# One decode kernel: the first pair's keys in one load, wo's row read by two engines, gu's half rows behind down's first block

## The chip, the core and the metric

The kernel runs on one core of one Trainium2 chip, whose other cores it leaves idle. The metric is device microseconds of one execution, the median of several. The kernel before takes 680.18 us (three runs, 679.79 to 680.27). One further execution was taken with the hardware profiler; its own time is 679.98 us and its span, first instruction to last, 678.2 us. All times of single instructions below are from that execution, counted from the start of its span.

## What is computed

One token passes through one transformer block whose two layer norms are scaled and shifted by a condition vector:

```python
mod = silu(c) @ w_mod                      # six rows of 640: sa, ca, ga, sb, cb, gb
h = layernorm(x) * (1 + ca) + sa
x = x + ga * A(h)                          # A: q = h @ wq; softmax(q k / sqrt(128)) v; @ wo
h = layernorm(x) * (1 + cb) + sb
x = x + gb * ((silu(h @ w_gate) * (h @ w_up)) @ w_down)
```

The width is 640. Attention has 32 heads of 128 with a cache of 16384 positions, and each head has its own keys and values, in bf16. Keys and values are 134 MB each, of 290 MB read in all. The feed-forward width is 1728, which is 13 chunks of 128 and one of 64.

## The kernel before, in words

**The plan.** All instructions are written as operations with an engine, a name and a list of operations that they depend on (`op` and `dma`, L77 and L83). Each engine gets its operations in the order in which the program names them, and waits on semaphores for those of other engines. So a wait on an engine holds up everything named later on that engine. All large loads are issued by SyncE (SP in the profile) at L90, one after another in the program's order, each one when its dependencies are met.

**Heads in pairs.** The 32 heads are 16 pairs. A pair's keys are 8192 KB, 64 KB on each of 128 partitions, and so are its values. There are two key buffers (`kring`, slots 0 and 1) and one value buffer (`vbuf`). The last pair's values go into key slot 0. Before the pairs start, `w_mod` lies in key slot 1 and `wq` in `vbuf`, so their users have to be done before K1 (pair 1's keys) and V0 (pair 0's values) can be loaded. K0 goes straight into slot 0.

**One pair.** VectorE (DVE) multiplies the keys by the query (mult) and folds the products in halves (fold). TensorE (PE) sums the remaining 16 columns against an identity (R). VectorE finds the largest score (pm), ScalarE (ACT) and TensorE spread it (d2, mx), VectorE takes the minimum (nb), and ScalarE does the exponential (exp, L602). Then TensorE multiplies by the values (pv, L518). A pair is worked in two parts. For pairs 1 to 14 (`score`, L549) the parts are halves of each head's 128 elements, so both need the whole load. For the first and the last pair (`score_end`, L567) the parts are the two halves of the positions, with the cut in `KCUT`.

**The order of the loads.** SyncE issues w_mod, wq, K0 in two loads of 4096 KB, K1, V0, and then K2, V1, K3, V2 and so on. K(p+1) waits until R of pair p-1 is done in both parts (its slot is free then), and V(p) waits until pv of pair p-1 is done. pv(p-1) stands in TensorE's order behind the first R of pair p, and this R needs the first mult and folds of pair p. VectorE's order over the first pairs is: mult and three folds of pair 0's first part, the same of its second part, mult of pair 1's first part, pm of pair 0, first fold, nb of pair 0, second fold, mult and folds of pair 1's second part, mult of pair 2.

**The tail.** Behind the last pair come wo's projection, the second layer norm, gate and up, and down. wo (L683 to L690) is 64 matmuls of 32 weight columns each: for each of 32 chunks one matmul with 512 columns into `wr_ps[0]` and one with 128 into `wr_ps[1]`, on four column groups of the array in turn. ScalarE copies both results into `wo_row` (L693), ten small matmuls (`wo_cols`, L699) turn the row into columns, and everything behind needs them. `gu` (L754) is the product of gate and up, `down` (L760 to L774) is five blocks of w_down: 16, 16, 16, 4 and 4 matmuls, each with its own load (wd0 to wd4). The last block is the chunk of 64, whose rows are spread over 128 partitions as half rows. `twice_gu` (L755, TensorE) and `gu_half` (L757, VectorE) make its factor.

Of the kernel before, what the change touches and what calls it, by code (L numbers as in the profile page):

```python
# [8 lines left out]
ALU = mybir.AluOpType  # L9
ACTF = mybir.ActivationFunctionType  # L10
# [27 lines left out]
class _Plan:  # L38
# [38 lines left out]
    def op(self, eng, fn, deps=(), name="", chan=None):  # L77
        o = _Op(eng, fn, list(deps), name, len(self.ops), self.loop.get(eng), chan)
        o.sig = chan is not None
        self.ops.append(o)  # L80
        return o

    def dma(self, out_ap, in_ap, key, deps=(), name="", eng="sp", noncontig=False):  # L83
        nc = self.nc

        def fn(e, out_ap=out_ap, in_ap=in_ap, noncontig=noncontig):
            if noncontig:
                with nc.allow_non_contiguous_dma(reason="tiny vector layout change"):
                    return e.dma_start(out_ap, in_ap)
            return e.dma_start(out_ap, in_ap)  # L90

        return self.op(eng, fn, deps, name, chan=self.dma_chan(key))
# [126 lines left out]
def build(nc, A_x, A_k, A_v, A_wq, A_wo, B_wg, B_wu, B_wd, c_in, w_mod, out):  # L219
    H, S, Dh = A_k.shape[1], A_k.shape[2], A_k.shape[3]  # L220
    D = A_x.shape[2]
# [4 lines left out]
    T2 = 2 * S // 128  # L226
# [4 lines left out]
    NF = 13  # L231
# [4 lines left out]
    FCH = NF + 1  # L236
# [6 lines left out]
    with es:  # L243
        block = es.enter_context(nc.Block())
        plan = _Plan(nc, es)
        op, dma = plan.op, plan.dma
        POOL, ACT, DVE, PE = "pool", "act", "dve", "pe"

        def sb(name, shape, dtype):
            return es.enter_context(nc.sbuf_tensor(name, list(shape), dtype))  # L250
# [62 lines left out]
        gu_col = sb("gu_col", [128, FCH], BF16)  # L313
        gu_half = sb("gu_half", [128, 2], BF16)
        even = sb("even", [128, 2], F32)
        twice = sb("twice", [128, 64, 2], BF16)
# [5 lines left out]
        wo_row = q_f[:, 0:2 * D].bitcast(F32)  # L322
# [11 lines left out]
        wr_ps = [psb[1], psb[6]]  # L334
        cx_ps = psb[4]
        A_ps = psb[6]
        attn_ps = psb[7]
# [23 lines left out]
            out=ident[:], in_=ones_bf[:], pattern=[[1, 128]], compare_op=ALU.is_equal,  # L361
# [27 lines left out]
        def layernorm_ops(src_f32, src_dep, sum_ap, c0, tag, xc_t, free=None, between=None):  # L389
# [26 lines left out]
            out=sel[:], in_=ident[:].rearrange("p (s r) -> p r s", s=4)[:, 0:8, :], axis=AX.X, op=ALU.add), deps=[o_ident], name="sel")  # L416
        o_msk = op(DVE, lambda e: e.tensor_reduce(
            out=msk[:], in_=ident[:].rearrange("p (j k) -> p j k", k=32), axis=AX.X, op=ALU.add), deps=[o_ident], name="msk")

        def f_e32(e):  # L420
# [3 lines left out]
        o_even = op(DVE, lambda e: e.tensor_reduce(  # L424
            out=even[:], in_=ident[:].rearrange("p (j k) -> p k j", k=2), axis=AX.X, op=ALU.add), deps=[o_ident], name="even")
        o_twice = op(DVE, lambda e: e.tensor_copy(out=twice[64:128], in_=ident[64:128, 64:128].unsqueeze(2).broadcast_to([64, 64, 2])), deps=[o_ident], name="twice")
# [4 lines left out]
        def wide(col):  # L431
            return col.broadcast_to([col.shape[0], 32])
# [11 lines left out]
        def pick(half, n, o_m, free):  # L444
# [13 lines left out]
            out=tt1[:], in0=modc[:, KC:2 * KC], scalar=1.0, in1=xn[:], op0=ALU.add, op1=ALU.mult),  # L458
            deps=[o_m0, o_xn], name="t1")
# [11 lines left out]
        for g in range(H // 4):  # L471
            b = g % 2
# [9 lines left out]
            for half in range(2):  # L482
                ps = slice(64 * half, 64 * half + 64)
                ev.append(op(ACT, lambda e, g=g, b=b, half=half, ps=ps: e.activation(
                    out=qbc[ps, 2 * g:2 * g + 2, :],
                    in_=q_ps[b][ps, :].rearrange("p (a h d) -> p a h d", a=2, h=2)[:, :, half, :], func=ACTF.Copy),
                    deps=[o_q[g]], name="qbc%d_%d" % (g, half)))
# [6 lines left out]
        KCUT = [0, T2 // 2, T2]  # L494
# [2 lines left out]

        def load_k(p):
            deps = [o_R[p - 2]] if p >= 2 else ([o_mod[1]] if p == 1 else [])
            cuts = KCUT if p == 0 else [0, T2]  # L500
            d_k[p] = [dma(kring[:, p % 2, a:b], k_src(p)[:, a:b], ("k", p % 2, c), deps=deps, name="dma_k%d_%d" % (p, c))
                      for c, (a, b) in enumerate(zip(cuts, cuts[1:]))]

# [106 lines left out]
        def step(p):  # L610
# [3 lines left out]
            diag(p - 1)  # L614

        load_k(0)
        load_k(1)
        load_v(0)
        reduce_end(0, 0, score_end(0, 0))
# [22 lines left out]
        f1 = score_end(PL, 1)  # L642
# [11 lines left out]
        for i, (b, r0, r1) in enumerate(DOWN):  # L654
            if b is None:
                dst, src = wt_v, B_wd[NF * 128:F, :].rearrange("q (h n) -> (q h) n", h=2)
            else:
# [7 lines left out]
                 deps=[o_exp[PL], o_rz, o_onesf, o_rstd], name="L")  # L665
# [5 lines left out]
            out=Z[:].rearrange("p (h j) -> p h j", j=4), in0=msk[:].unsqueeze(1).broadcast_to([128, H, 4]),  # L671
            in1=on_f[:].unsqueeze(2).broadcast_to([128, H, 4]), op=ALU.mult), deps=[o_on, o_msk], name="z")
        o_am = op(PE, lambda e: e.matmul(A_ps[:, 0:H], lhsT=Z[:], rhs=e32[:], start=True, stop=True),
                  deps=[o_z, o_e32] + o_qev[-2], name="am")
# [3 lines left out]
            out=Z[:].rearrange("p (j k) -> p j k", k=32), in_=msk[:].unsqueeze(2).broadcast_to([128, 4, 32])), deps=[o_msk, o_am], name="strips")  # L678

        def project(c):  # L680

            def f_wo(e):
                last = None  # L683
                for k in range(WCUT[c], WCUT[c + 1]):
                    r = k % 4
                    for ps, a, b in ((wr_ps[0], 0, 512), (wr_ps[1], 512, D)):
                        last = e.matmul(ps[32 * r:32 * r + 32, 0:b - a], lhsT=wide(A_sb[:, k:k + 1]), rhs=wo_v[:, k, a:b],  # L687
                                        start=(k < 4), stop=(k >= H - 4), tile_position=(0, 32 * r))
                return last
            return op(PE, f_wo, deps=[o_as, d_wo[c], o_exp[NP - 2]] + o_qev[-1], name="wo%d" % c)  # L690
        for c in range(len(WCUT) - 1):
            o_p = project(c)
        o_wr = [op(ACT, lambda e, a=a, b=b, ps=ps: e.activation(out=wo_row[:, a:b], in_=ps[:, 0:b - a], func=ACTF.Copy),  # L693
                   deps=[o_p, f1], name="wo_row%d" % a) for ps, a, b in ((wr_ps[0], 0, 512), (wr_ps[1], 512, D))]

        def f_cols(e):
            last = None
# [9 lines left out]
        o_abf = op(DVE, lambda e: e.tensor_copy(out=attn_bf[:], in_=attn_ps[:, 0:KC]), deps=[o_wo], name="attn_bf")  # L707
        o_ga = op(DVE, lambda e: e.tensor_tensor(out=tt2[:], in0=attn_bf[:], in1=ga, op=ALU.mult), deps=[o_abf, o_m0], name="ga_attn")
        o_x1 = op(DVE, lambda e: e.scalar_tensor_tensor(
            out=x1[:], in0=tt2[:], scalar=1.0, in1=x_f32[:], op0=ALU.mult, op1=ALU.add, accum_out=st[:, 4:5]),  # L710
            deps=[o_ga, o_xf], name="x1")
# [18 lines left out]
        def gate0(o_xc1):  # L730
# [5 lines left out]
            out=tt3[:], in0=xc1[:], scalar=st[:, 7:8], in1=onep_b[:], op0=ALU.mult, op1=ALU.mult),  # L736
            deps=[o_xc1, o_rstd1, o_onep_b], name="t2")
# [3 lines left out]
            out=x1_sp.rearrange("p (r k) -> p r k", k=KC), in0=x1[:].unsqueeze(1).broadcast_to([128, 32, KC]),  # L741
            in1=e32[:].unsqueeze(2).broadcast_to([128, 32, KC]), op=ALU.mult), deps=[o_x1, o_e32, o_diag[PL]], name="x1_sp")
        o_xr = op(PE, lambda e: e.matmul(xr_ps[:, 0:RW], lhsT=Z[:], rhs=x1_sp, start=True, stop=True),
                  deps=[o_xsp, o_ot[PL], o_strips], name="x1_rows")
# [7 lines left out]
        o_sg = op(DVE, lambda e: e.tensor_tensor(out=sg[:], in0=g_sb[:], in1=rg[:], op=ALU.mult), deps=[o_rg, o_gs], name="sg")  # L752
        o_x1r = op(ACT, lambda e: e.activation(out=x1_row, in_=xr_ps[:, 0:RW], func=ACTF.Copy), deps=[o_xr], name="x1_row")
        o_gum = op(DVE, lambda e: e.tensor_tensor(out=gu_col[:], in0=u_ps[:, 0:FCH], in1=sg[:], op=ALU.mult), deps=[o_sg, o_u], name="gu")  # L754
        o_tw = op(PE, lambda e: e.matmul(attn_ps[:, 8:9], lhsT=twice[64:128].rearrange("p q h -> p (q h)"), rhs=gu_col[64:128, NF:FCH], start=True, stop=True),  # L755
                  deps=[o_gum, o_twice, o_abf], name="twice_gu")
        o_guh = op(DVE, lambda e: e.tensor_tensor(out=gu_half[:], in0=attn_ps[:, 8:9].broadcast_to([128, 2]), in1=even[:], op=ALU.mult),  # L757
                   deps=[o_tw, o_even], name="gu_half")

        for i, (b, r0, r1) in enumerate(DOWN):  # L760

            if b is None:
                work = [(gu_half[:, r // 2:r // 2 + 1], wt_v[:, RW * (r % 2):RW * (r % 2) + RW], r) for r in range(4)]
            else:
                j0 = BLOCKS[b][2]
                work = [(gu_col[:, j:j + 1], wd_v[:, j, RW * r:RW * r + RW], r) for j in range(j0 + r0, j0 + r1) for r in range(4)]

            def f_down(e, i=i, work=work):
                last = None
                for at, (col, rows, r) in enumerate(work):  # L770
                    last = e.matmul(f_ps[32 * r:32 * r + 32, 0:RW], lhsT=wide(col), rhs=rows, start=(i == 0 and at < 4),  # L771
                                    stop=(i == len(DOWN) - 1 and at >= len(work) - 4), tile_position=(0, 32 * r))
                return last
            prev = op(PE, f_down, deps=[o_gum if b is not None else o_guh, d_wd[i], o_nb[PL]], name="down%d" % i)  # L774
        o_t3 = op(DVE, lambda e: e.tensor_tensor(out=tt_row, in0=f_ps[:, 0:RW], in1=gb_row[:], op=ALU.mult), deps=[prev, o_gb], name="gb_ffn")
        o_or = op(DVE, lambda e: e.tensor_tensor(out=o_row[:], in0=tt_row, in1=x1_row, op=ALU.add), deps=[o_t3, o_x1r], name="o_row")
        o_dst = out[0, 0].rearrange("(r n) -> r n", r=4)
# [51 lines left out]
```

## Time and profile before

| What | Value |
|---|---|
| Median of three runs | 680.18 us (679.79 to 680.27) |
| The profiled execution's own time | 679.98 us |
| Its span | 678.2 us |
| VectorE busy | 513.0 us (76%) |
| TensorE busy in matmuls | 366.2 us (54%) |
| ScalarE busy | 46.7 us (7%) |
| HBM read | 290.47 MB, 428 GB/s over the span |
| The queue that carries the loads (q1) | 99.2% of 16 engines' span |

The landing of one load is its issue (timeline of SyncE) plus the time from issue to landing that the view of the issuing line gives for that issue alone:

| Load | Issued | Issue to landing | Landed |
|---|---|---|---|
| w_mod, 4800 KB | 0.8 | 14.2 | 15.0 |
| wq, 5120 KB | 1.3 | 25.9 | 27.2 |
| K0, first 4096 KB | 1.73 | 35.1 | 36.9 |
| K0, second 4096 KB | 2.2 | 45.4 | 47.6 |
| K1, 8192 KB | 19.3 | 47.7 | 67.0 |
| V0, 8192 KB | 38.9 | 47.5 | 86.4 |
| K2, 8192 KB | 74.0 | 31.8 | 105.8 |
| V1, 8192 KB | 99.2 | 25.9 | 125.1 |
| K3, 8192 KB | 108.5 | 36.0 | 144.5 |
| V2, 8192 KB | 134.0 | 29.8 | 163.8 |

How to read it: the 16 DMA engines work through the loads in the order of issue. An issue whose time to landing is well over what its bytes take has waited behind others, which means that the engines had work all along.

### The profile page before, as it was taken

Reading aid. Unit: us, or ns where it says so; the run is one execution under the profiler, and the core shown is the slowest. Engines: PE = TensorE matmul, PEld = TensorE weight load, DVE = VectorE, ACT = ScalarE, POOL = GpSimd, SP = SyncE. Lnnn points to the kernel's source line nnn. Section 1 sums busy time; section 2 is a strip of 40 time slices with the busy share of each in tenths; the row PEclk is TensorE's granted clock in tenths of the full one; section 3 lists DMA queues with packets and bytes.
Section 4 is the critical chain, followed back from the end, with each engine's and each line's share of the span. In section 5 each row is a group of like instructions: output and inputs, shape, how many; then the busy total and the mean of one; then the engine's idle time right before and its main releaser. Section 6 shows DMA issues by size and latency. Waiting matters only on the chain.

```text
span 678.2 us, 5410 instructions
## 1 busy us (share of the span) xinstructions
PE 366.2 (54%) x2068; PEld 146.5 (22%) x2069; DVE 513.0 (76%) x185; ACT 46.7 (7%) x147; POOL 0.7 (0%) x6
## 2 busy tenths in 40 slices
PE   2522275755728274664818375572818465471677
PEld 1111122221312122221302122121212222130236
DVE  2189997959596896959597795959699695959812
ACT  1120000100000000000000010000000000000011
POOL 0000000000000000000000000000000000000000
PEclk9675565655657565565757555575756556575765
DMA  9999999999999999999999999999999999999997
GB/s 372 442 459 433 433 433 430 433 430 433 437 430 433 433 433 433 433 437 433 433 433 433 437 433 433 433 433 433 433 433 433 433 433 433 433 437 433 434 402 305
DMA packets 6355, 290.58 MB, mean 428 GB/s; under 512 B 714, under 2 KB 972, under 8 KB 1484
## 3 DMA queue, kind: packets, MB, share of 16 engines
q1 hardware_dynamic: 6340, 290.48, 99.2%
q8 instruction: 5, 0.08, 0.0%
q10 hardware_dynamic: 8, 0.00, 0.0%
q14 instruction: 2, 0.02, 0.0%
HBM read 290.47 MB, written 0.00 MB: 428 GB/s over the span
## 4 chain that ended last, share of the span: by engine, by line
DMA 48%; DVE 28%; issue 13%; PE 11%; DVEq 0%; ACT 0%; SPq 0%
DMA kring<-in_A_k_cache_dram 45%; DVE kring L554 10%; PE psb L544 7%; DVE kring L559 6%; DVE kring L570 4%; DVE kring L576 3%; DMA vbuf<-in_A_wo_dram 3%; DVE kring L564 3%; PE psb L518 1%; PE psb L724 1%; PE psb L687 1%; PE psb L584 1%; PE psb L699 0%; PE psb L771 0%; DVE pm L590 0%
## 5 line engine op out<-in xcount | busy, mean ns | idle before, releaser
L554 DVE TENSOR_TENSOR kring<-kring,qbc 128x16384 bf16<-128x16384 bf16 x28 | 243.2, 8687 | 96.2 <-DMA kring<-in_A_k_cache_dram 96.2
L544 PE MATMUL psb<-kring,ident 128*128 x448 | 197.5, 607 | 119.3 <-DVE kring L564 119.3
L559 DVE TENSOR_TENSOR kring<-kring 128x8192 bf16<-128x8192 bf16 x28 | 123.8, 4420 | 0.5
L544 PEld LDWEIGHTS psb<-kring,ident 128*128 128x128 bf16 x448 | 53.9, 120 | 247.1 <-issue 246.0
L518 PE MATMUL psb<-vbuf,PZ 128*8 128x512 bf16 x960 | 82.6, 520 | 0.0
L594 PE MATMUL psb<-d,bd_f 128*128 128x64 f32 x32 | 11.0, 446 | 122.0 <-ACT d L592 122.0
L564 DVE TENSOR_TENSOR kring<-kring 128x4096 bf16<-128x4096 bf16 x28 | 64.0, 2286 | 0.5
L570 DVE TENSOR_TENSOR kring<-kring,qbc 128x16384 bf16<-128x16384 bf16 x4 | 34.8, 8688 | 23.4 <-DMA kring<-in_A_k_cache_dram 23.4
L518 PEld LDWEIGHTS psb<-vbuf,PZ 128*8 128x8 bf16 x960 | 27.0, 109 | 60.2 <-issue 51.5
L584 PE MATMUL psb<-kring,ident 128*128 128x128 bf16 x64 | 14.5, 392 | 40.3 <-DVE kring L576 40.3
L594 PEld LDWEIGHTS psb<-d,bd_f 128*128 128x128 f32 x32 | 8.0, 311 | 124.1 <-DVE pm L590 114.4
L576 DVE TENSOR_TENSOR kring<-kring 128x8192 bf16<-128x8192 bf16 (+2 forms) x12 | 31.7, 2645 | 0.3
L533 PEld LDWEIGHTS psb<-sel,acc_sb 128*128 128x128 f32 x128 | 28.5, 311 | 8.4 <-issue 4.3
L533 PE MATMUL psb<-sel,acc_sb 128*128 128x2 f32 x128 | 25.6, 322 | 1.4 <-ACT acc_sb L524 1.4
L524 ACT ACTIVATE acc_sb<-psb 128x512 f32<-128x512 f32 x16 | 9.6, 597 | 212.0 <-PE psb L518 212.0
L602 ACT ACTIVATE PZ<-psb,nb 64x256 bf16<-64x256 f32 x32 | 15.0, 469 | 64.8 <-DVE nb L598 64.6
L584 PEld LDWEIGHTS psb<-kring,ident 128*128 128x128 bf16 x64 | 7.4, 122 | 46.7 <-DVE kring L576 41.6
L592 ACT ACTIVATE d<-negid,pm 128x64 f32<-128x64 f32 x16 | 5.6, 348 | 153.9 <-DVE pm L590 153.9
L477 PE MATMUL psb<-vbuf,h_col 128*128 128x512 bf16 x39 | 11.2, 461 | 8.3 <-DMA vbuf<-in_A_wq_dram 8.3
L537 ACT ACTIVATE OT_sb<-psb 128x2 f32 (+1 forms) x16 | 2.8, 172 | 151.3 <-PE psb L533 151.3
L590 DVE TENSOR_REDUCE pm<-psb 128x1 f32<-128x256 f32 x16 | 6.7, 418 | 3.7 <-PE psb L584 3.7
L477 PEld LDWEIGHTS psb<-vbuf,h_col 128*128 128x128 bf16 x40 | 4.3, 116 | 15.6 <-DMA vbuf<-in_A_wq_dram 8.8
(104 smaller groups left out, 80.4 us busy)
## 6 DMA issues: line engine op xcount, KB each, us to landing
kring<-in_A_k_cache_dram SPq DMA_DIRECT2D x2, 4096.0 KB, 40.3
vbuf<-in_A_wq_dram SPq DMA_DIRECT2D x1, 5120.0 KB, 25.9
kring<-in_w_mod_dram SPq DMA_DIRECT2D x1, 4800.0 KB, 14.2
vbuf<-in_A_wo_dram SPq DMA_DIRECT2D x1, 4480.0 KB, 23.0
kring<-in_B_w_gate_dram SPq DMA_DIRECT2D x1, 2160.0 KB, 18.7
kring<-in_B_w_up_dram SPq DMA_DIRECT2D x1, 2160.0 KB, 23.5
kring<-in_B_w_down_dram SPq DMA_DIRECT2D x3, 640.0 KB, 25.7
vbuf<-in_A_wo_dram SPq DMA_DIRECT2D x1, 640.0 KB, 24.2
```

Of the source, the lines that this page charges most:

```text
L477: last = e.matmul(q_ps[b][:, 0:512], lhsT=h_col[:, k:k + 1].broadcast_to([128, 128]), rhs=wq_v[:, k, g * 512:(g + 1) * 512], start=(k == 0 ...
L518: last = e.matmul(acc_ps[32 * s:32 * s + 8, :], lhsT=PZ[:, j, :], rhs=v_at(p)[:, 4 * j:4 * j + 4, :].rearrange("p t d -> p (t d)"), start= ...
L533: last = e.matmul(OT_ps[:, 0:2], lhsT=acc_sb[:, 128 * i:128 * (i + 1)], rhs=sel[:, i:8:4], start=(i == 0), stop=(i == 3))
L544: last = e.matmul(S_ps[:, 0:T2], lhsT=ident[:], rhs=kring[:, bass.ds(plan.slot(p), 1), :, d].rearrange("p o t -> p (o t)"), start=(d == 0) ...
L554: return e.tensor_tensor(out=kv4, in0=kv4, in1=q4, op=ALU.mult)
L559: o_f = op(DVE, lambda e: e.tensor_tensor(out=kv4[:, :, 0], in0=kv4[:, :, 0], in1=kv4[:, :, 1], op=ALU.add), deps=[o_m], name="fold%d_%d" ...
L564: return op(DVE, lambda e: e.tensor_tensor(out=lo[:, :, 0:QR], in0=lo[:, :, 0:QR], in1=lo[:, :, QR:QW], op=ALU.add), deps=[o_f], name="fol ...
L570: o = op(DVE, lambda e: e.tensor_tensor(out=kv, in0=kv, in1=qbc[:, p, :].unsqueeze(1).broadcast_to([128, KCUT[c + 1] - KCUT[c], 128]), op= ...
L576: o = op(DVE, lambda e, w=w: e.tensor_tensor(out=kv[:, :, 0:w], in0=kv[:, :, 0:w], in1=kv[:, :, w:2 * w], op=ALU.add), deps=[o], name="fol ...
L584: last = e.matmul(S_ps[:, KCUT[c]:KCUT[c + 1]], lhsT=ident[:], rhs=kring[:, p % 2, KCUT[c]:KCUT[c + 1], d], start=(d == 0), stop=(d == 15))
L594: o_mx[p] = op(PE, lambda e: e.matmul(mx_ps[:, 0:64], lhsT=bd_f[:], rhs=d2[:], start=True, stop=True), deps=[o_d2, o_bd1, o_bd2, o_nb[p - ...
L602: o_exp[p] = op(ACT, lambda e, half=half, ps=ps: e.activation(out=PZ[ps, :, 4 * half:4 * half + 4], in_=S_ps[ps, 0:T2].rearrange("p (c i) ...
```

## The change

Three edits. K0 is one load of 8192 KB instead of two of 4096 KB; its two parts are still computed one after the other with the cut of `KCUT`, and both now wait for the one load. wo's two results are 320 columns each, the first copied by ScalarE and the second by VectorE, instead of 512 and 128 columns that ScalarE copies one after the other. `twice_gu` and `gu_half` are named behind down's first block instead of ahead of it.

```diff
         def load_k(p):
             deps = [o_R[p - 2]] if p >= 2 else ([o_mod[1]] if p == 1 else [])
-            cuts = KCUT if p == 0 else [0, T2]
+            cuts = [0, T2]
             d_k[p] = [dma(kring[:, p % 2, a:b], k_src(p)[:, a:b], ("k", p % 2, c), deps=deps, name="dma_k%d_%d" % (p, c))
                       for c, (a, b) in enumerate(zip(cuts, cuts[1:]))]
...
-                    for ps, a, b in ((wr_ps[0], 0, 512), (wr_ps[1], 512, D)):
+                    for ps, a, b in ((wr_ps[0], 0, D // 2), (wr_ps[1], D // 2, D)):
                         last = e.matmul(ps[32 * r:32 * r + 32, 0:b - a], lhsT=wide(A_sb[:, k:k + 1]), rhs=wo_v[:, k, a:b],
                                         start=(k < 4), stop=(k >= H - 4), tile_position=(0, 32 * r))
...
-        o_wr = [op(ACT, lambda e, a=a, b=b, ps=ps: e.activation(out=wo_row[:, a:b], in_=ps[:, 0:b - a], func=ACTF.Copy),
-                   deps=[o_p, f1], name="wo_row%d" % a) for ps, a, b in ((wr_ps[0], 0, 512), (wr_ps[1], 512, D))]
+        o_wr = [op(ACT, lambda e: e.activation(out=wo_row[:, 0:D // 2], in_=wr_ps[0][:, 0:D // 2], func=ACTF.Copy), deps=[o_p, f1], name="wo_row0"),
+                op(DVE, lambda e: e.tensor_copy(out=wo_row[:, D // 2:D], in_=wr_ps[1][:, 0:D // 2]), deps=[o_p, f1], name="wo_row1")]
...
-        o_tw = op(PE, lambda e: e.matmul(attn_ps[:, 8:9], lhsT=twice[64:128].rearrange("p q h -> p (q h)"), rhs=gu_col[64:128, NF:FCH], start=True, stop=True),
-                  deps=[o_gum, o_twice, o_abf], name="twice_gu")
-        o_guh = op(DVE, lambda e: e.tensor_tensor(out=gu_half[:], in0=attn_ps[:, 8:9].broadcast_to([128, 2]), in1=even[:], op=ALU.mult),
-                   deps=[o_tw, o_even], name="gu_half")
-
         for i, (b, r0, r1) in enumerate(DOWN):
...
             prev = op(PE, f_down, deps=[o_gum if b is not None else o_guh, d_wd[i], o_nb[PL]], name="down%d" % i)
+            if i == 0:
+                o_tw = op(PE, lambda e: e.matmul(attn_ps[:, 8:9], lhsT=twice[64:128].rearrange("p q h -> p (q h)"), rhs=gu_col[64:128, NF:FCH], start=True, stop=True),
+                          deps=[o_gum, o_twice, o_abf], name="twice_gu")
+                o_guh = op(DVE, lambda e: e.tensor_tensor(out=gu_half[:], in0=attn_ps[:, 8:9].broadcast_to([128, 2]), in1=even[:], op=ALU.mult),
+                           deps=[o_tw, o_even], name="gu_half")
```

## The prediction

> **What bounds the kernel now.** I read the page's slices first, then its chain of work, then the timeline of the first pairs beside the landings of single loads, last the timeline of the end. From the page:
>
> ```profile
> DMA  9999999999999999999999999999999999999997
> GB/s 372 442 459 433 433 433 430 433 430 433 437 430 433 433 433 433 433 437 433 433 433 433 437 433 433 433 433 433 433 433 433 433 433 433 433 437 433 434 402 305
> ...
> q1 hardware_dynamic: 6340, 290.48, 99.2%
> ...
> DMA 48%; DVE 28%; issue 13%; PE 11%; DVEq 0%; ACT 0%; SPq 0%
> ```
>
> The DMA engines are busy in every slice at one rate: 290 MB at 433 GB/s are 671 us of the 678. DVE's 28% of the chain doesn't contradict this; it is where the backward walk meets keys that had landed. The landings say the same: K1, V0, K2, V1, K3 and V2 land at 67.0, 86.4, 105.8, 125.1, 144.5 and 163.8, 19.3 to 19.4 us apart. So 8192 KB cost 19.35 us of stream, and no hole lies between them. Whatever makes a hole in this stream adds its whole length to the end, as long as nobody has slack behind it; whatever only makes an engine faster adds nothing until the last load.
>
> What keeps the stream full is that each load is issued before the one ahead of it has landed. The timeline of the first pairs shows where that is tightest:
>
> ```profile
> 36.89 8.69 DVE L570 TENSOR_TENSOR kring<-kring,qbc 128x16384 bf16<-128x16384 bf16 x1 [16.02 <-DMA kring<-in_A_k_cache_dram]
> 45.62 8.01 DVE L576 TENSOR_TENSOR kring<-kring 128x8192 bf16<-128x8192 bf16 x3
> 53.55 8.68 DVE L570 TENSOR_TENSOR kring<-kring,qbc 128x16384 bf16<-128x16384 bf16 x1
> 62.27 8.01 DVE L576 TENSOR_TENSOR kring<-kring 128x8192 bf16<-128x8192 bf16 x3
> 70.19 8.68 DVE L554 TENSOR_TENSOR kring<-kring,qbc 128x16384 bf16<-128x16384 bf16 x1
> ...
> 98.97 2.29 DVE L564 TENSOR_TENSOR kring<-kring 128x4096 bf16<-128x4096 bf16 x1
> 105.77 8.69 DVE L554 TENSOR_TENSOR kring<-kring,qbc 128x16384 bf16<-128x16384 bf16 x1 [4.50 <-DMA kring<-in_A_k_cache_dram]
> ```
>
> ```profile
> 73.99 0.33 SPq L90 DMA_DIRECT2D kring<-in_A_k_cache_dram  x1
> 99.18 0.33 SPq L90 DMA_DIRECT2D vbuf<-in_A_v_cache_dram  x1
> ```
>
> DVE waits 16 us for K0's first half and then runs without a gap from 36.89 to 101.26. K2's issue (73.99, end of pair 0's second R) and V1's (99.18, end of pv0) hang on this run of work: first mult to V1's issue is 62.3 us. V1 was issued 6.6 us before K2 landed at 105.8. That is all the slack there is. From pair 2 on DVE waits for keys (4.5 us here; 7 to 8 us in every later pair), so later loads have more.
>
> **Part 1, K0 in one load.** It removes one DMA issue on SP (0.58 us, while the queue is full: worth nothing) and adds a wait: the first mult needs all of K0. Queued behind that mult is all of the run above, and TensorE's R and pv wait for DVE. K0's second half landed at 47.6 and the same bytes lie ahead of it, so I let the one load land there: the first mult starts at 47.6 instead of 36.89, **10.7 us later**. K1 had landed 3.2 us before DVE took it, and all durations in between are DVE's and TensorE's own, so nothing is caught up: K2 is issued at 84.7, V1 at 99.2 + 10.7 = 109.9.
>
> K2: V0 lands at 86.4, so this issue comes at the edge; at worst K2 takes the 22.2 us worked out below from its issue and lands at 106.9. Its reader, mult of pair 2, can't start before DVE's run ends at 101.26 + 10.7 = 112.0, which hides that.
>
> V1: the queue is empty from 105.8 (or 106.9) to 109.9, and V1 then starts on idle engines. The trace has one large load on idle engines, w_mod: 14.2 us for 4800 KB, of which 4800/8192 x 19.35 = 11.35 are stream, so 2.85 are start and completion. A floor are the two output writes, 0.6 KB each, issued at 676.57, with the span over at 678.2: 1.6 us. I take 2.85, since w_mod is the row of the same kind. V1 lands at 109.9 + 2.85 + 19.35 = 132.1 instead of 125.1: **+7.0 us**.
>
> The Trainium skill, "DMA: Bandwidth & Descriptors", section "Anatomy of one DMA — SWDGE (gpsimd) path", gives about 2.0 us of fixed cost plus bytes over 436 GB/s for a transfer issued by GpSimd. As an estimate, V1 would take 21.2 us by it and the sum below would be 685.8; w_mod's row, a load of this kernel on this queue, speaks for the dearer start.
>
> Does it last to the end? K3 is issued at about 119, well inside V1's load, and lands 19.35 us behind it, at 151.5. Pair 2's mult starts at 112.0 (6.2 us late), so V2 (before: 134.0) comes at about 140.3 and K4 (before: 144.1) at about 150.3, each before the load ahead of it has landed (151.5 and 170.8). No second hole; and from K3 on each key load lands 7.0 us late and DVE waits for it, up to the last pair:
>
> ```profile
> 608.87 8.69 DVE L570 TENSOR_TENSOR kring<-kring,qbc 128x16384 bf16<-128x16384 bf16 x1 [7.42 <-DMA kring<-in_A_k_cache_dram]
> ```
>
> So the whole tail moves by 7.0. The bounds of this term: 5.75 with the floor of 1.6; one more us off if K0 lands earlier (first rival); 7.9 if an instruction fetch falls into V1's load. The packet records show those of queue q8 at 42.1 and 105.9, 16 KB each, holding one DMA engine for 1.06 and 0.89 us, and a load lands with its slowest engine.
>
> **Part 2, wo's row on two engines.** In the tail's timeline and the groups by shape:
>
> ```profile
> 663.24 0.77 ACT L693 ACTIVATE qbc<-psb 128x512 f32<-128x512 f32 x2 [4.59 <-PE psb L687]
> 664.06 2.28 PEld L699 LDWEIGHTS psb<-ind,qbc 128*128 128x128 f32 x10 [1.47 <-ACT qbc L693]
> ...
> 673.83 1.92 PE L771 MATMUL psb<-kring,gu_col 128*32 128x160 bf16 x52
> 675.54 0.35 PE L771 MATMUL psb<-kring,gu_half 128*32 128x160 bf16 x4
> ```
>
> The two ACT copies take 0.77 us together. 320 columns on ACT lie between its 160 (0.285, L753) and 512 (0.598): 0.44. On DVE no plain copy of 320 f32 out of PSUM is in the trace; L446 reads 320 there in 0.48 with a second operand, L775 160 in 0.32, so 0.40 to 0.48. They run side by side: 0.77 - 0.48, **0.3 us earlier** at wo_cols. Behind the new DVE copy two memsets are queued (0.15 us), needed by gate and up 4 us later: free. The matmuls stay 64 with 640 columns a chunk; a step of eight takes 0.53 us now, 1.2 columns per ns, pv's step of 512 columns runs at the same rate (0.43), down's 160 at 1.08. So no change, at worst 8 x 0.06 = 0.5 us dearer.
>
> **Part 3, gu's half rows later.** down0 starts at gu's end, 0.1 us earlier; twice_gu then costs the same 0.1 on PE between down0 and down1. gu_half (0.16, DVE, with only the end queued behind) must be done before down4, over 1 us later. Its worth by itself is 0; it lets down0 run while later blocks land.
>
> **Parts 2 and 3 at the end.** down0 could start 0.4 earlier, at 673.4. But issue and time to landing give wd2 at 674.7, wd3 at 675.2 and wd4 at 675.3, and down4 starts at 675.46 now. The last load lets at most some 0.2 through: **-0.2 us** (0 to -0.4, as wd4 moves against the compute). Up, in between, isn't held: wu landed at 670.1, up starts at 670.9, 670.6 after.
>
> **Sum.** 679.98 + 7.0 - 0.2 = 686.8 for the profiled execution's like. It lies 0.2 below the median 680.18, inside the runs' spread; I predict **686.9 us**, 1.0% slower.
>
> **Rivals.** (1) K0 lands sooner as one load. Its two halves took 47.6 - 27.2 = 20.4 us behind wq, a whole load takes 19.35. If the extra 1.05 belongs to the cut, K0 lands at 46.6, every step from the first mult on is 1 us earlier, V1 lands at 131.1: 685.8. For it: the number. Against it: the fetch at 42.1 held one engine 1.06 us, as long as the excess, and a fetch stays. The same page and section by its rule would put the saving at the fixed cost of one transfer, 2.0 us, and the time at 684.9 as an estimate; loads 19.35 us apart show no such cost between queued loads.
> (2) Not slower: the delay fits into the slack and the tail's gain is left, 679.8. This needs V1 issued 2.85 us before K2's end, by about 103, so a first mult no more than 3.8 us late, at 40.7 or before. It decides at V1's issue. Against it: the second half's 9.7 us of stream can't land by then, and DVE has no gap to catch up in.
> (3) wo's equal parts run worse on the four column groups, and a fetch delays V1: 686.9 + 0.5 + 0.9 = 688.3. Nothing speaks for it but the bounds.
>
> **Chances.** Forecast 0.62, (1) 0.22, (2) 0.04, (3) 0.12. The range goes from floor and early landing together (7.0 - 1.05 - 1.25 - 0.4: 684.3) to (3), 688.3. About 0.2%, 1.4 us, is what a measurement can tell from no change: faster 0.01, same 0.03, slower 0.96.
>
> **What would show it.** Right: the first mult near 47.6, V1's issue near 109.9, one slice around 107 to 112 with DMA idle, V1 landing near 132, then 19.35 us between loads and DVE waiting for keys as before; wo_row's two copies side by side in under 0.5 us; down4 starting just behind wd4's landing. Wrong: V1 issued before K2 lands, a second hole behind V2, or DVE no longer waiting for keys at the last pair, in which case the loss was caught up.

## The result, and the profile after

The changed kernel takes **687.13 us** (median of five runs, 686.76 to 688.08) against 680.06 us (679.79 to 680.27) for the kernel before beside it: a ratio of 1.0106, 95% interval [1.0091, 1.012]. The profiled execution took 687.13 us, with a span of 685.3 us instead of 678.2: +7.1 us. Where they are can be read from three views. First the page, its slices and the load queue:

```profile
DMA  9999997999999999999999999999999999999997
GB/s 380 458 426 428 390 409 307 428 432 448 448 437 432 428 428 432 428 432 428 428 444 448 436 440 428 428 428 432 428 432 428 432 440 448 432 440 432 426 403 304
...
q1 hardware_dynamic: 6196, 290.48, 98.3%
```

The same bytes, and one slice, the seventh (103 to 120 us), in which the DMA engines were not busy throughout. The queue's share fell from 99.2% to 98.3% of a longer span. The timelines of DVE and of SyncE say what came late:

```profile
47.56 8.69 DVE L570 TENSOR_TENSOR kring<-kring,qbc 128x16384 bf16<-128x16384 bf16 x1 [26.70 <-DMA kring<-in_A_k_cache_dram]
...
111.85 8.68 DVE L554 TENSOR_TENSOR kring<-kring,qbc 128x16384 bf16<-128x16384 bf16 x1
```

```profile
84.67 0.33 SPq L90 DMA_DIRECT2D kring<-in_A_k_cache_dram  x1
109.11 0.33 SPq L90 DMA_DIRECT2D vbuf<-in_A_v_cache_dram  x1
119.16 0.33 SPq L90 DMA_DIRECT2D kring<-in_A_k_cache_dram  x1
```

The first mult starts 10.7 us later (47.56 instead of 36.89), and with it K2's issue (84.67 instead of 73.99) and V1's (109.11 instead of 99.18). DVE has no wait any more ahead of pair 2's mult (111.85): K2 was there, DVE came late. In the table of stretches of 2 us, the last three numbers of a row are the granted clock (the share of its full speed that TensorE's clock was given), the share of the DMA engines and GB/s; a packet, 2.4 us long here, counts where it starts:

```profile
102.00:104.00 2.00, 2.00 (x8) 0.38 (x7) 2.00 (x1) 0.00 (x0) 0.00 (x0) 0.50 1.21 524
104.00:106.00 2.00, 2.00 (x21) 0.63 (x24) 1.97 (x2) 0.00 (x0) 0.00 (x0) 0.50 0.00 0
106.00:108.00 2.00, 2.00 (x32) 0.73 (x28) 2.00 (x1) 0.00 (x0) 0.00 (x0) 0.76 0.00 0
108.00:110.00 2.00, 1.05 (x20) 0.27 (x12) 1.97 (x2) 0.60 (x1) 0.00 (x0) 1.00 0.00 0
110.00:112.00 2.00, 0.00 (x0) 0.00 (x0) 2.00 (x2) 0.00 (x0) 0.00 (x0) 1.00 1.57 524
```

Three stretches without a new packet, until V1's first ones at 110. The same three in the kernel before:

```profile
104.00:106.00 2.00, 2.00 (x6) 0.60 (x5) 0.23 (x1) 0.00 (x0) 0.00 (x0) 0.50 0.63 270
106.00:108.00 2.00, 2.00 (x6) 0.64 (x5) 2.00 (x1) 0.00 (x0) 0.00 (x0) 0.50 0.77 328
108.00:110.00 2.00, 1.97 (x10) 1.76 (x8) 2.00 (x1) 0.00 (x0) 0.00 (x0) 0.50 1.15 492
```

In the packet records (every single DMA packet with its start, duration and size) the last packet of K2 ends at 105.96 and the first of V1 starts at 110.08. V1 landed at 132.2 (109.1 and 23.1 from issue to landing), 7.1 us after the 125.1 of before; K3 at 151.6, V2 at 170.9, K4 at 190.3, each 19.4 us apart again; and the last pair's mult starts at 616.00 instead of 608.87, still behind a wait of 7.41 us for its keys. So by the landings all of the 7.1 us are there when V1 lands, and nobody behind it has slack to win them back. The packet records, under "pv ahead of the first R" below, split them: 2.0 us arise already ahead of K2, and 5.1 ahead of V1.

The tail as the profile has it:

```profile
668.83 0.44 ACT L693 ACTIVATE qbc<-psb 128x320 f32<-128x320 f32 x1 [3.76 <-PE psb L687]
668.83 0.49 DVE L694 COPY qbc<-psb 128x320 f32<-128x320 f32 x1 [3.73 <-PE psb L687]
...
677.21 2.44 PE L724 MATMUL psb<-h_col,kring 128*128 128x1 bf16 x70 [0.68 <-DMA kring<-in_B_w_up_dram]
...
681.90 0.86 PE L766 MATMUL psb<-kring,gu_col 128*32 128x160 bf16 x20 [0.43 <-DMA kring<-in_B_w_down_dram]
682.62 0.33 PE L766 MATMUL psb<-kring,gu_half 128*32 128x160 bf16 x4
```

wo_row's copies run side by side (0.49 us instead of 0.77), but up now waits for w_up, and down's third block for w_down. The last add (o_row) starts at 683.35 instead of 676.30: 7.05 later, where the last pair was 7.13 late. The tail gave 0.08 us.

### The profile page after: what moved, and what is told of

It is laid out like the page before. It is cut to its first block, busy times and chain, and to the rows that moved or that the text cites. A ratio compares the mean times of both kernels' runs of the same rounds, so it can differ in the third digit from the quotient of the medians.

```text
span 685.3 us, 5411 instructions
## 1 busy us (share of the span) xinstructions
PE 360.5 (53%) x2068; PEld 144.9 (21%) x2069; DVE 513.5 (75%) x186; ACT 46.4 (7%) x146; POOL 0.7 (0%) x6
## 3 DMA queue, kind: packets, MB, share of 16 engines
q1 hardware_dynamic: 6196, 290.48, 98.3%
## 4 chain that ended last, share of the span: by engine, by line
DMA 44%; DVE 34%; issue 13%; PE 8%; SPq 0%; DVEq 0%; ACT 0%
DMA kring<-in_A_k_cache_dram 41%; DVE kring L554 13%; DVE kring L559 8%; PE psb L544 7%; DVE kring L570 5%; DVE kring L576 5%; DMA kring<-in_B_w_down_dram 4%; DVE kring L564 3%; PE psb L584 1%; SPq L90 0%; DVE pm L590 0%; DVE nb L598 0%; PE psb L533 0%; PE psb L766 0%; DVEq L191 0%
## 5 line engine op out<-in xcount | busy, mean ns | idle before, releaser
L518 PE MATMUL psb<-vbuf,PZ 128*8 128x512 bf16 x960 | 79.3, 502 | 0.0
L477 PE MATMUL psb<-vbuf,h_col 128*128 128x512 bf16 x39 | 10.7, 444 | 8.8 <-DMA vbuf<-in_A_wq_dram 8.8
```

The costliest lines, as they stand in the source:

```text
L477: last = e.matmul(q_ps[b][:, 0:512], lhsT=h_col[:, k:k + 1].broadcast_to([128, 128]), rhs=wq_v[:, k, g * 512:(g + 1) * 512], start=(k == 0 ...
L518: last = e.matmul(acc_ps[32 * s:32 * s + 8, :], lhsT=PZ[:, j, :], rhs=v_at(p)[:, 4 * j:4 * j + 4, :].rearrange("p t d -> p (t d)"), start= ...
```

## The experiments

The theory: all of the loss is the hole in the stream of loads ahead of V1, because V1's issue hangs on the first mult by 62 us of work; the tail's edits gain nothing, because the last loads set the end. Rivals: the large load itself is dearer; the tail's edits cost something; a late start of DVE costs as such, in proportion. Each ratio is to the kernel before, run beside it on the same chip (medians of 680.0 to 680.1).

**One load alone** (the `cuts` line of the change, nothing else).

> K0 in one load, everything else as before. Theory (the whole loss is the hole in the stream of loads ahead of V1; the two edits of the tail only wait for w_down's blocks): 687.2 us, V1 issued near 109 and landing near 132. Rival (the tail's edits cost something of their own): the loss is smaller here, 686.5 or less. Rival (the tail's edits saved the forecast 0.2): 687.4.

687.28 us (686.87 to 687.97), ratio 1.0106 [1.0091, 1.0122]; first mult at 47.59, V1 issued at 109.2, landed at 132.4. The loss is there in full without the tail's edits. Its interval, 686.2 to 688.3 us, can't tell whether these cost or save some tenths; they are tried by themselves below.

**Two loads, but a late wait.**

```diff
-                deps=[d_k[p][min(c, len(d_k[p]) - 1)]] + o_qev[p // 2], name="mult%d_%d" % (p, c))
+                deps=[d_k[p][-1]] + o_qev[p // 2], name="mult%d_%d" % (p, c))
```

> K0 stays in two loads, but pair 0's first mult waits for the second one. Theory (the wait alone costs, not the shape of the load): first mult at 47.6, V1 issued near 109 to 110, 687.2 us. Rival (the load of 8192 KB itself is dearer, or shifts the DMA engines against each other): 680.1, as before.

686.91 us (686.43 to 688.04), ratio 1.0103 [1.0088, 1.0119]; first mult at 47.60, V1 issued at 109.00:

```profile
47.60 8.69 DVE L570 TENSOR_TENSOR kring<-kring,qbc 128x16384 bf16<-128x16384 bf16 x1 [26.91 <-DMA kring<-in_A_k_cache_dram]
```

```profile
109.00 0.33 SPq L90 DMA_DIRECT2D vbuf<-in_A_v_cache_dram  x1
```

The wait costs, not the load's size: all of K0 is there by 47.6 with one load and with two.

**The tail's edits alone** (the change without its `cuts` line).

> K0 in two loads, wo's equal parts and gu's late spread as in the change. Theory (the end is bound by the landing of w_down's last blocks): 679.9 to 680.1, with a wait for w_down ahead of down's third block. Rival (the compute chain of the tail sets the end): wo_row's 0.3 us comes through, 679.7.

679.91 us against 680.04, ratio 0.9999 [0.999, 1.0008]: not to be told from nothing. The profile shows why:

```profile
673.66 0.72 PE L766 MATMUL psb<-kring,gu_col 128*32 128x160 bf16 x16
...
674.54 0.54 PEld L766 LDWEIGHTS psb<-kring,gu_col 128*32 128x32 bf16 x20 [0.48 <-DMA kring<-in_B_w_down_dram]
```

The second block ran at 673.66. In the kernel before it came near 674.4 (an estimate: 673.83 and 16/52 of the 1.92 us of 52 matmuls). The gain was there, and the third block then stood until its load had landed (674.5).

**wo's equal parts alone.**

> Only wo's equal parts, read by ScalarE and VectorE. Theory: the two copies take 0.49 us side by side instead of 0.77 one after the other, and the wait for w_up or w_down takes it back: 680.0. The 64 matmuls of wo take 4.47 us if the granted clock is 0.5 in their stretch and about 3.3 if it is 0.9, in either cut. Rival (equal parts themselves make the matmuls faster): 3.3 us at a clock of 0.5.

679.97 us against 680.06, ratio 0.9998 [0.9989, 1.0007]; the copies took 0.49 us. wo's matmuls took 3.78 us, at a granted clock of 0.96 for the first 0.9 us and 0.50 for the other 2.9. Counted in time at 0.5, that is 0.86 x 1.92 + 2.9 = 4.6, against 4.47 in the kernel before at 0.50 throughout; the changed kernel's 3.31 us at 1.00, 0.87, 0.50 give 4.6 as well. So the granted clock accounts for the difference, and the cut for none that can be seen.

**pv ahead of the first R**, on top of the whole change: the first mult stays late, V1's issue doesn't.

```diff
-            reduce_mm(p, 0, score(p, 0, before(p)))
+            f = score(p, 0, before(p))
             pv(p - 1)
+            reduce_mm(p, 0, f)
```

> The change, and in TensorE's order pv of the pair before stands ahead of the first R instead of behind it. The first mult still starts at 47.6. Theory (the loss is V1's late issue): exp of pair 0 is done near 95.4, pv0 near 101, V1 is issued near 101 instead of 109.1, 5 us ahead of K2's landing, no hole: 679.9 to 680.8. Rival (a start of VectorE that is 10.7 us late costs by itself, or K2's late issue at 84.7 does): 686 to 687, as without the reordering.

681.95 us (681.78 to 682.17), ratio 1.0027 [1.0016, 1.0039].

```profile
47.42 8.69 DVE L570 TENSOR_TENSOR kring<-kring,qbc 128x16384 bf16<-128x16384 bf16 x1 [26.75 <-DMA kring<-in_A_k_cache_dram]
```

```profile
84.52 0.33 SPq L90 DMA_DIRECT2D kring<-in_A_k_cache_dram  x1
101.32 0.33 SPq L90 DMA_DIRECT2D vbuf<-in_A_v_cache_dram  x1
```

The first mult is as late as ever, and 5.2 of the 7.1 us are gone, with V1's issue at 101.3; so neither DVE's late start nor the large load costs by itself. But 1.9 us stayed, over a us more than expected. I had taken K2's late issue to be covered, by its landing. The landing is that of the slowest DMA engine, and one of the 16 trails by about 1 us. Each engine ends its share of a load with a packet of 4 bytes in the packet records; the mean of these 16 ends tells the stream:

| Mean end of the 16 engines' shares | V0 | K2 | V1 | K3 |
|---|---|---|---|---|
| before | 84.39 | 103.76 | 123.27 | 142.60 |
| changed | 84.35 | 105.79 | 130.38 | 149.72 |
| changed, pv ahead of R | 84.21 | 105.67 | 125.09 | 144.42 |
| the same, K2 in halves (next but one) | 84.18 | 103.58 | 124.42 | 143.75 |

K2's issue at 84.5 to 84.7 already made a hole, and K2's mean end comes 1.9 to 2.0 us later than before: 15 engines had ended V0 by 84.6 to 84.8. In the changed kernel these 2.0 us are part of the 7.1, and 5.1 come on top ahead of V1; when V1's hole is closed, K2's is left.

**Smaller delays of the first mult.** K0 in two loads with the cut at 5/8 (shown), 3/4 or 7/8; the computation keeps its halves.

```diff
-            cuts = KCUT if p == 0 else [0, T2]
+            cuts = [0, 5 * T2 // 8, T2] if p == 0 else [0, T2]
```

> K0 in two loads of 5/8 and 3/8 (5120 and 3072 KB); pair 0's first mult waits for the first. It starts near 39.3, 2.4 us later than with halves. Theory (V1 must be issued some 2.9 us ahead of K2's landing at 105.8, so about 3.7 us of delay are free): no loss, 680.1, V1 issued near 101.6. Rival (every us of delay of VectorE's start costs, 7 us for 10.7): 681.7.

> First load 3/4 (6144 KB). First mult near 41.7 to 42.7, 4.8 to 5.8 us later. Theory: the free 3.7 us are used up, the loss is what is over, 1.1 to 2.1 us, up to 0.9 more if an instruction fetch meets V1: 681.2 to 683.0. Rival (proportional): 683.3 to 683.9. Rival (only the full wait costs): 680.1.

> First load 7/8 (7168 KB). First mult near 44.2 to 45.2, 7.3 to 8.3 us later. Theory: 3.6 to 4.6 us of loss, up to 0.9 more with a fetch: 683.7 to 685.6. Rival (proportional): 684.9 to 685.5, so this size alone doesn't tell; together with 5/8 and 3/4 it gives the line, whose foot is at 3.7 us by theory and at 0 by the rival.

| First load | First mult, delay | V1 issued | Time (runs) | Loss |
|---|---|---|---|---|
| 1/2 (before) | 36.89, 0 | 99.2 | 680.06 (679.70 to 680.42) | 0 |
| 5/8 | 39.05, 2.2 | 100.6 | 681.04 (679.87 to 682.65) | 1.0 |
| 3/4 | 42.72, 5.8 | 104.6 | 682.69 (681.10 to 683.17) | 2.6 |
| 7/8 | 44.97, 8.1 | 106.6 | 685.13 (684.48 to 685.41) | 5.1 |
| all (the change) | 47.56, 10.7 | 109.1 | 687.13 (686.76 to 688.08) | 7.1 |

The times at 3/4 and 7/8 lie in their theory's ranges, and 3/4 lies above the 680.1 of "only the full wait costs" and below the proportional range, so the loss is neither. From 3/4 on it grows by 4.4 us over 4.8 us of delay, and that line has its foot at 5.8 - 2.6/0.92 = 3.0 us. It can't tell 3.0 from the 3.7 us of theory: the interval of the 3/4 run's ratio, 1.0022 to 1.0045, is a loss of 1.5 to 3.1 us, which alone moves the foot from 4.5 to 2.1. 5/8 missed (ratio 1.0016 [1.0007, 1.0025]): between no loss and 2.6 us from run to run, in one profile without a hole. Two more runs, on another chip, asked why; the first is the plain 5/8 cut again, as its text says.

> MISLABELLED: this file is the 5/8 cut without the reordering, a repeat of the 5/8 run. Theory (its runs lie between no hole and a hole ahead of V1, from run to run): again 679.9 to 682.7, median near 681.0. Rival (the spread of the first time was the chip's): all runs within 0.5 of one another.

680.43 us (679.97 to 681.07), ratio 1.0007 [0.9998, 1.0016]: less than the first time, and between the two expectations. It is again not one value: 5 of its 11 runs lie above 680.47, the highest of the 27 runs of the kernel before beside them.

> First load of K0 5/8, and pv of the pair before ahead of the first R. Theory (the spread of the 5/8 run is V1's issue at the edge of K2's end): V1 is issued some 8 us earlier, near 93, and the spread goes: 679.9 to 680.2, within 0.6 of one another. Rival (it is something else about a later start of VectorE, K2's issue near 76 for one): median near 681.0 with a spread of over 2 us, as before.

680.11 us (679.67 to 680.36), ratio 1.0001 [0.9992, 1.001]. With the same late start of DVE, no run lies above 680.47 any more, and the spread is gone. The two issues, in the timeline of SyncE of the 5/8 run and then of this one:

```profile
100.58 0.33 SPq L90 DMA_DIRECT2D vbuf<-in_A_v_cache_dram  x1
```

```profile
92.27 0.33 SPq L90 DMA_DIRECT2D vbuf<-in_A_v_cache_dram  x1
```

So at 5/8 V1's issue stands at the edge. No profile fell on one of the dear runs, so how late V1 was in them isn't shown. A candidate is pv0, at whose end V1 is issued: in the profiles of these kernels it took from 4.84 us (the repeat, at a mean granted clock of 0.74) to 6.34 us (K2 in halves, below, at 0.56). It starts near 95.4 here, so the longest would put V1's issue near 101.7. That is an estimate, seen in no run.

**K2 in halves**, on top of pv ahead of R: its first half is issued when pair 0's first R has read that half of the slot.

```diff
-            cuts = [0, T2]
-            d_k[p] = [dma(kring[:, p % 2, a:b], k_src(p)[:, a:b], ("k", p % 2, c), deps=deps, name="dma_k%d_%d" % (p, c))
+            cuts = KCUT if p == 2 else [0, T2]
+            d_k[p] = [dma(kring[:, p % 2, a:b], k_src(p)[:, a:b], ("k", p % 2, c), deps=[o_R0a] if p == 2 and c == 0 else deps, name="dma_k%d_%d" % (p, c))
...
-                     deps=[d_k[p][-1]] + o_qev[p // 2], name="mult%d_%d" % (p, c))
+                     deps=d_k[p] + o_qev[p // 2], name="mult%d_%d" % (p, c))
...
-        reduce_end(0, 0, score_end(0, 0))
+        o_R0a = reduce_end(0, 0, score_end(0, 0))
```

> As the run with pv ahead of the first R (681.95), and K2 is loaded in two halves: the first is issued when pair 0's first R has read its half of the slot (near 68), the second behind the second R as before (84.5). Theory (what was left there, 1.9 us, is a second, smaller hole ahead of K2: 15 of 16 DMA engines end V0 at 83.9 to 84.6 and get K2's first packets at 85.5): no hole, 680.0 to 680.8 (up to 0.8 for where instruction fetches fall). Rival (the rest is a fetch into V1's load, or VectorE's late start): 681.5 to 682.

680.40 us (679.77 to 682.89), ratio 1.0009 [1.0, 1.0018]. K0 is still one load and the first mult starts at 47.53, and the loss is nearly gone: by the medians 1.55 of the 1.9 us went with K2's hole. What is left differs from run to run. The profiled run (681.05) had V1 issued at 102.0, behind a pv0 of 6.34 us, and by the table above it lost about 1.3 us there (124.42 - 103.58 = 20.8 us instead of 19.5), though K2's first engine ended only at 103.2: some engines waited, and V1's first packets took 2.5 to 2.9 us on most of them instead of 2.42. So in this profile an issue 1.2 us ahead of the first engine's end was too late, and in that of 5/8 one 2.6 us ahead (100.6 and 103.2) was in time.

**Halves, the tail's edits and pv ahead of R together.**

> K0 in two halves as before, the two edits of the tail, and pv of the pair before ahead of the first R. Theory (the stream of loads is full and its last landing sets the end): 679.9, as with the tail edits alone (679.91), and no run above 680.4. Rival (V1 at the edge now and then costs the kernel before some tenths, which pv ahead would save): 679.6 or less.

680.07 us (679.68 to 680.31) against 679.99, ratio 1.0001 [0.9992, 1.001]. No version beats the kernel before: its stream is full.

## Why the prediction was right, step by step

- **The bound and the mechanism** held: a stream without slack, V1's issue tied to the first mult, one slice in which the DMA engines stood, 7.1 us to the end. Shown by pv ahead of R (the same late mult, most of the loss gone) and by the late wait with two loads (the same loss).
- **The first mult** at 47.6 (forecast 47.6). Rival 1 falls: the one load landed at 47.5, and the excess over 19.35 us isn't the cut's. A fetch of 16 KB held one engine for 1.01 us at 40.8, and in the packet records that engine ends K0 at 47.09, the 15th at 46.11. The Trainium skill, "Runtime: NRT & Kernel Launch", section "Instruction fetch mechanics", says that instruction memory is refilled in blocks of 16 KiB, at a cost mostly hidden. The size agrees; in this stream the fetch leaves one engine about 1 us behind for the loads after it.
- **V1's issue** at 109.1, forecast 109.9: pv0 took 5.07 us instead of 5.84, at a mean granted clock of 0.72 instead of 0.62 over it (the two products are 3.6 us both). The forecast had taken its duration as fixed.
- **V1's start on idle engines**, forecast 2.85 us, was 23.1 - 19.35 = 3.75: 0.97 from issue to first packet, first packets of 2.95 to 3.45 us where later ones take 2.42, and a fetch of 0.88 us at 118.2. The bounds named the fetch; the value taken left it out. These two misses, -0.8 and +0.9, cancelled by luck in the 132.1 us that came out as 132.2.
- **K2's late issue** was called hidden. That held for DVE (K2 landed at 106.3, its reader came at 111.85) and for the sum, which went by V1's issue, later still. It isn't free: the loss is two holes, 2.0 us ahead of K2 and 5.1 ahead of V1, and the first was seen once the second was closed.
- **Rival 2's point** ("V1 issued by about 103") was too kind. The first engines run dry at 103.2 to 103.4, not at the landing 105.8, and an issue at 102.0 was already late. So the 6.6 us of slack are 4.2 by the first engine (99.2 to 103.4), and V1's issue can be late by something between 1.4 and 2.8 us (in time at 100.6, late at 102.0, from 99.2), not by 3.8.
- **The tail**, forecast -0.2, gave 0.08 in the profile and nothing that the medians resolve alone. "Up isn't held" failed: with the faster pv and wo matmuls the compute came 1.5 us ahead of the loads (wo_row 5.6 us later than before, the loads 7.1), and up waited 0.68 us. wo's equal parts, rival 3, cost nothing on the column groups.

## What to carry to other kernels

In a stream of loads that is full, look for the issue that has least time ahead of the stream's end, and follow what it waits for back to its first wait: a merged load that delays this first wait costs what goes beyond that slack, while all that it saves is one issue (0.58 us on SyncE, with the queue full). The Trainium skill, "Perfetto Trace Analysis", section "DMA Optimizations", says that splitting loads may help where DMA engines are generally idle. Here the load queue was busy for 99.2% of the span, and the split was still worth 7.1 us, because the work on the first half opens the chain that frees the buffers of K2 and V1. Read the slack from the first engine to run dry, not from the landing, which is the slowest engine's, and leave a lead: 1.2 us was too little here, 2.6 enough.

## What the runs showed that was not expected

One DMA engine of the 16 can trail the others by 1 us through many loads after a single fetch of 16 KB (V0: 15th engine 84.84, last 85.94; K2: 104.21 and 105.28), and a hole lets it catch up (changed kernel, K2: 105.94 and 105.96). And the granted clock of TensorE, not the shape of the work, accounts for 3.3 to 4.5 us for the same 64 matmuls of wo and for 5.07 or 5.84 us for pv0. wo's did not move the time, since the last loads set the end. pv0's does where V1's issue is late: V1 is issued at its end, and the 0.8 us that it was shorter in the changed kernel came off the hole.
